# Moving batch bursts and folds to other slots of a spectral-filter and GELU kernel written out slot by slot

## The chip, the cores and the metric

The kernel runs on one core of a Trainium2 chip. The metric is the device time of one execution in microseconds (us). Five engines are at work: TensorE (PE) multiplies matrices and writes its results to PSUM, VectorE (DVE) and ScalarE (ACT) read PSUM and do elementwise work, GpSimd (POOL) builds tables and issues transfers, and SyncE (SP) issues transfers. Each engine works through its own list of instructions, and semaphores tie the lists together.

## The reference

A batch of 8 sequences of 3008 tokens with 256 channels is filtered along the sequence in the frequency domain. The filtered tokens then go through a two-layer network with an exact GELU between the layers.

```python
X = np.fft.rfft(x, axis=1)                  # x: 8 x 3008 x 256
Y = X * (filt_r + 1j * filt_i)[None]        # filter: 1505 x 256
y = np.fft.irfft(Y, n=x.shape[1], axis=1)
h = y.reshape(24064, 256) @ w_in            # 256 x 2048
g = 0.5 * h * (1.0 + erf(h / sqrt(2)))
out = g @ w_out                             # 2048 x 256, float32 out
```

## The kernel before

**Two streams share the engines.** The dense stream takes the 24064 tokens in 47 tiles of 512 tokens. For a tile, `mm1` (line 634) makes 16 blocks of the hidden layer and ACT applies the GELU to each (line 637). The second product is done by a seven-product scheme on quarters of the matrices, `mm2_seven` (line 707): 112 matmuls in seven groups m = 0 to 6 of 16, numbered n = 0 to 111. DVE forms the sums of quarters which it needs: `sums_1` (line 676), `sums_2` (line 682) and `sums_3` (line 689). Group m = 2 (n = 32 to 47) needs `sums_2`: its first half needs the first call, and n = 36 needs the second. DVE also adds up the results out of PSUM: after m = 0 (line 722), m = 2 (lines 724, 727), m = 4 (lines 729, 730, 733) and m = 6 (line 736). The results lie in the PSUM pool `o`, which has two banks. A new bank is taken at m = 0, m = 1, m = 3 and m = 5, so the bank that m = 1 of a tile takes at n = 16 must first have been emptied by line 736 of the tile before it.

The other stream filters the batches, by a transform of 3008 = 47 x 64 points in stages. For each batch b from 1 to 7:
- `fold` (lines 106, 107), four calls: DVE adds and subtracts the two halves of a quarter of the loaded input.
- `s1` (line 428), four bursts of 8 matmuls; DVE (line 331) and ACT (line 329) each copy two of the four PSUM banks to `a_sb`; SP stores it to a scratch array R in DRAM, and `r1` (line 444) loads it back in another order as `b_sb`.
- `s2` (line 457), three bursts u = 0 to 2 of 16 matmuls; `s2_out` (line 469), four calls for each burst: DVE multiplies the four banks by the filter F into `p`.
- `s3` (line 483), three bursts; it reads what the four `s2_out` calls of its u wrote. ACT empties its four banks into `v_sb` (line 329), half with the burst and half one slot later in `s3_out`; SP stores `v_sb` to a second scratch array (line 496), and `r2` (line 503) loads it back as `d_sb`.
- `s4` (line 512), sixteen bursts of 4 matmuls, numbered by a group u = 0 to 7 and a half; ACT or DVE puts the result into the ring of tokens `y_sb`, which `mm1` reads.
Bursts take one bank of the PSUM pool `h` and three of the pool `f`, which has three banks.

**The order is written out by hand.** No planner reorders the work: the kernel runs under a manual schedule. A loop runs over slots s = 0, 1, 2, ..., 16 slots for each tile. In a slot the loop first calls what has been put there with `put(slot, function, ...)`, in the order of the `put` calls; then 7 matmuls of `mm2_seven` for the tile before (tile t - 1); then one `mm1` of tile t. So each engine's list follows the slots. In the slots of tile 0 there is only `mm1` beside the bursts. Tile 5 (slots 80 to 95) needs the first tokens of batch 1; there the loop does 14 matmuls of `mm2_seven` in each of the first six slots, and starts with `mm1` at slot 86.

The plan for batch b is made around `hi = first(b)`, the first slot of the tile that needs the batch's first token: 80 for b = 1, 176 for b = 2, 656 for b = 7. `s1`, `n1`, `r1` are the first slot of the s1 bursts, their distance and the slot of `r1`; `s2` holds the three slots of the s2 bursts. The s2_out calls follow at +0, +2, +4, +6, s3 at +10 and s3_out at +11. `load_next` puts the loads of the next batch's input (POOL, line 98) behind s2_out calls of this batch: a small copy on POOL, the gate (line 149), waits for the `p` of an s2_out. `after[b]` is the slot of the first `r2`, and `busy` holds slots which s4 bursts keep clear of.

For batch 1 the s4 bursts of u = 0 lie at slots 83 and 84 and those of u = 1 at 86 and 87. The stores of tiles 0 to 2 go through SP and those of later tiles through POOL. Batch 0 goes another way, before slot 0, which begins at about 38.0 us.

Of the kernel before, what the change touches and what calls it, by code (L numbers as in the profile page):

```python
# [775 lines left out]
def kernel(  # L776
# [9 lines left out]
    m = _Mix(ctx, tc, x, filt_r, filt_i, moe_w_in, moe_w_out, out)  # L786
    nc, B, S = tc.nc, m.B, m.S
# [116 lines left out]
    def put(slot, f, *a):  # L904
        at.setdefault(slot, []).append((f, a))

    def first(b):
        return (b * S // TCH) * 16

    busy, crowd, after = set(), set(), {}  # L910
    for b in range(1, B):
        hi = first(b)
        e = 4 * (b == B - 1)
        s1, n1, r1 = (1, 4, 16) if b == 1 else (hi - 87, 3.7, hi - 73) if b == 2 else (hi - 94 - e, 3.7, hi - 80 - e)
        s2 = (32, 46, 58) if b == 1 else (hi - 64 - 2 * e, hi - 48 - 3 * e, hi - 32 - 3 * e)
        busy.update(range(s1 - 1, s1 + int(3 * n1) + 2))
        for c in range(4):
            slot = s1 + int(c * n1)
            put(slot - 1 if b == 1 else s1 - 28 + 6 * c, m.fold, b, c)
            put(slot, m.s1, b, c)  # L920
            put(r1 if c < 3 else s2[0] + 1, m.r1, b, c)
        for u in range(3):
            put(s2[u], m.s2, b, u)
            for i in range(4):
                put(s2[u] + 2 * i, m.s2_out, b, u, i // 2, i % 2)
            put(s2[u] + 10, m.s3, b, u)
            put(s2[u] + 11, m.s3_out, b, u, 1)
            busy.update(range(s2[u] - 1, s2[u] + 5), range(s2[u] + 9, s2[u] + 12))
        after[b] = s2[2] + 15
        crowd.update(range(s2[0], after[b]), range(s1 + 66, s1 + 94))  # L930
        if b + 1 < B:
            for i, (u, o, p) in enumerate(((0, 5, 2), (0, 7, 2), (1, 1, 4), (1, 5, 6), (1, 7, 6), (2, 1, 8), (2, 5, 10), (2, 7, 10))):
                put(s2[u] + o, m.load_next, b, p, i // 2, i % 2)

    for b in range(1, B):
        end = 1000000
        if b == B - 1:
            s4 = first(b) - 17
            for u in range(16):
                put(s4 + u, m.s4, b, u // 2, u % 2, act if u % 2 else False)  # L940
            for c in range(4):
                put(after[b] if c < 3 else s4 + 5, m.r2, b, c)
            continue
        for u in range(7, -1, -1):
            due = (b * S + GRP * u) // TCH * 16
            end = min(end, due - 2 + 6 * (u == 0 and b == 1))
            for half in (1, 0):
                while end in busy:
                    end -= 1
                assert end > after[b] + 7  # L950
                put(end, m.s4, b, u, half, act if half or end in crowd or b == 1 and u == 0 else False)
                busy.add(end)
                end -= 1 if u < 3 else 2
            if u % 2 == 0:
                put(after[b] if u == 0 else end - 11, m.r2, b, u // 2)
# [8 lines left out]
    for i, slot in enumerate((10, 80, 96, 112)):  # L964
        put(slot, m.table_4_all, parts[2 * i:2 * i + 2])
    put(1, m.load_filters_again, nc.gpsimd, 0, 8)
    put(17, m.load_filters_again, nc.sync, 8, 16)
    put(19, m.weight_sums)
    seven = range(1, NT)
    for t in seven:  # L970
        for i, s in enumerate((12, 13, 15, 16 if t == S // TCH - 1 else 17)):
# [49 lines left out]
```

## Time and profile before

| what | value |
|---|---|
| time, median of 3 runs | 751.81 us (750.87 to 752.24) |
| the profiled execution | 750.82 us, span 749.0 us |
| PE busy | 724.9 us (97%) |
| DVE busy | 581.7 us (78%) |
| ACT busy | 574.7 us (77%) |
| POOL busy | 287.6 us (38%) |
| granted TensorE clock | full throughout |
| HBM traffic | 141 GB/s over the span |

PE's busy share is a share of the whole span. The matmuls overlap one another, so it doesn't say how near PE is to its peak; it says that PE seldom stands still. What matters here is where it does: the view of waits names, for each engine, the engine and line that ended its idle time, and the timeline shows the instructions around such a wait. A wait in one place may have its cause in a long queue on the engine that ended it.

### The profile page before, as it was taken

What the parts mean: (1) busy time and instruction counts of PE and PEld (TensorE: products, weight loads), DVE (VectorE), ACT (ScalarE), POOL (GpSimd) and SP (SyncE); (2) the same over time, 40 slices, a digit from 0 to 9 for tenths busy, and PEclk for the clock granted to TensorE, in tenths of its full rate; (3) what the DMA queues carried; (4) which work ended last, traced back from release to release, by engine and by line L of the source; (5) the groups of instructions that cost most, each with busy time, mean ns of one, the idle gap of its engine ahead of it and who ended that gap; (6) DMA issues with size and microseconds to landing.
All of it is one profiled execution on the core that took longest, in us unless ns stands there. A gap on an engine that the chain in (4) does not pass through costs nothing.

```text
span 749.0 us, 20863 instructions
## 1 busy us (share of the span) xinstructions
PE 724.9 (97%) x8450; PEld 507.4 (68%) x8588; DVE 581.7 (78%) x1034; ACT 574.7 (77%) x1050; POOL 287.6 (38%) x540
## 2 busy tenths in 40 slices
PE   7989999999999999999999999999999999999997
PEld 4846665666777667666677666666667766777776
DVE  7976797888887788778976889768887887676566
ACT  6986776777887788778887777877778787777773
POOL 7894325676122553134521354115531121112121
PEclk9999999999999999999999999999999999999999
DMA  9999652746346653656436456265545442401011
GB/s 148 221 208 222 144 117 74 208 106 124 86 116 182 121 115 87 154 139 135 105 108 169 107 117 152 71 156 136 110 101 127 143 111 84 111 30 57 30 58 57
DMA packets 84378, 90.79 MB, mean 121 GB/s; under 512 B 13290, under 2 KB 63466, under 8 KB 84154
## 3 DMA queue, kind: packets, MB, share of 16 engines
q1 hardware_dynamic: 61594, 49.63, 26.1%
q0 software_dynamic: 22272, 39.63, 23.9%
q8 instruction: 67, 1.10, 0.7%
q14 instruction: 29, 0.24, 0.1%
q10 hardware_dynamic: 416, 0.20, 0.1%
HBM read 57.15 MB, written 48.23 MB: 141 GB/s over the span
## 4 chain that ended last, share of the span: by engine, by line
PE 84%; ACT 5%; DVE 3%; DMA 3%; issue 2%; POOL 1%; DVEq 0%; SPq 0%; POOLq 0%
PE ps_o L707 36%; PE ps_h L634 36%; PE ps_s L483 3%; ACT g_sb L637 3%; PE ps_s L512 3%; PE ps_s L428 2%; DMA x_sb<-in_x_dram 2%; PE ps_s L457 1%; ACT v_sb L329 1%; PE ps_o L648 1%; DVE s_sb L676 1%; DMA F<-in_filt_i_dram 1%; ACT y_sb L329 1%; DMA b_sb<-R 1%; PE ps_c L581 0%
## 5 line engine op out<-in xcount | busy, mean ns | idle before, releaser
L637 ACT ACTIVATE g_sb<-ps_h 128x512 f16<-128x512 f32 x752 | 446.4, 604 | 150.9 <-PE ps_h L634 133.1
L634 PE MATMUL ps_h<-y_sb,w_in_sb 128*128 128x512 bf16 (+3 forms) x1466 | 416.5, 365 | 1.1 <-ACT g_sb L637 0.6
L754 POOL DMA_DIRECT2D out_dram<-ost x221 | 125.3, 574 | 397.7 <-DVE ost L736 389.1
L707 PEld LDWEIGHTS <-g_sb 128*128 128x128 f16 x2944 | 193.4, 98 | 87.6 <-issue 11.2
L707 PEld LDWEIGHTS <-s_sb 128*128 128x128 f16 x2208 | 147.9, 98 | 62.2 <-issue 11.3
L707 PE MATMUL ps_o<-w_sums,g_sb 128*128 128x128 f16 x1472 | 127.9, 219 | 3.1 <-DVE g_sb L682 2.2
L634 PEld LDWEIGHTS <-w_in_sb 128*128 128x128 bf16 x1600 | 124.9, 98 | 8.6 <-issue 2.5
L707 PE MATMUL ps_o<-w_sums,s_sb 128*128 128x128 f16 x1472 | 126.0, 219 | 1.8
L676 DVE TENSOR_TENSOR s_sb<-g_sb 128x1024 f16<-128x1024 f16 x184 | 120.4, 688 | 3.3 <-ACT g_sb L637 3.3
L707 PE MATMUL ps_o<-w_out_sb,g_sb 128*128 128x128 f16 x1472 | 119.1, 219 | 3.5 <-DVE ost L736 1.9
L469 DVE TENSOR_TENSOR p<-ps_s,F 128x1024 bf16<-128x1024 f32 x84 | 102.5, 1220 | 6.7 <-PE ps_s L457 5.3
L98 POOL DMA_DIRECT2D x_sb<-in_x_dram x156 | 79.0, 513 | 0.7 <-PE ps_c3t L596 0.4
L729 DVE TENSOR_TENSOR t_sb<-t_sb,ps_o 128x256 f32<-128x256 f32 x46 | 19.4, 421 | 64.9 <-PE ps_o L707 64.8
L682 DVE TENSOR_TENSOR g_sb<-s_sb,g_sb 128x1024 f16<-128x1024 f16 x92 | 65.1, 708 | 0.7
L689 DVE TENSOR_TENSOR s_sb<-g_sb 128x1024 f16<-128x1024 f16 x92 | 64.5, 701 | 0.0
L707 PE MATMUL ps_o<-w_out_sb,s_sb 128*128 128x128 f16 x736 | 63.9, 219 | 0.4
L329 ACT ACTIVATE y_sb<-ps_s 128x376 bf16<-128x376 f32 x95 | 47.3, 497 | 5.1 <-PE ps_s L512 5.1
L736 DVE TENSOR_TENSOR ost<-t_sb,ps_o 128x256 f32<-128x256 f32 x90 | 33.8, 417 | 21.9 <-PE ps_o L707 21.9
L512 PEld LDWEIGHTS <-d_sb 96*128 96x128 bf16 x448 | 31.9, 98 | 25.5
L331 DVE CAST a_sb<-ps_s 128x512 bf16<-128x512 f32 x54 | 34.8, 686 | 16.3 <-PE ps_s L428 16.0
L329 ACT ACTIVATE v_sb<-ps_s 128x512 bf16<-128x512 f32 x84 | 45.5, 597 | 0.2
L724 DVE TENSOR_TENSOR ost<-t_sb,ps_o 128x256 f32<-128x256 f32 x46 | 19.2, 418 | 26.9 <-PE ps_o L707 26.9
(154 smaller groups left out, 523.9 us busy)
## 6 DMA issues: line engine op xcount, KB each, us to landing
out_dram<-ost POOLq DMA_DIRECT2D x123, 128.0 KB, 2.7
b_sb<-R SPq DMA_DIRECT2D x28, 384.0 KB, 4.3
R<-v_sb SPq DMA_DIRECT2D x84, 128.0 KB, 2.4
d_sb<-R SPq DMA_DIRECT2D x56, 192.0 KB, 4.2
R<-a_sb SPq DMA_DIRECT2D x108, 96.0 KB, 2.2
x_sb<-in_x_dram POOLq DMA_DIRECT2D x48, 94.0 KB, 2.7
x_sb<-in_x_dram POOLq DMA_DIRECT2D x48, 48.0 KB, 2.7
x_sb<-in_x_dram POOLq DMA_DIRECT2D x12, 188.0 KB, 5.1
```

Source lines behind the costliest of these rows:

```text
L98: self.nc.gpsimd.dma_start(out=xt[64 * v + to:64 * v + to + m, h, 4 * c:4 * c + 4 * n, :], in_=xv[h][at:at + m, w:w + 4 * n, :])
L329: self.nc.scalar.activation(out=out, in_=in_, func=AF.Copy, scale=1.0 if scale is None else scale)
L331: self.nc.vector.tensor_copy(out=out, in_=in_)
L469: self.nc.vector.tensor_tensor(out=self.st[b, "w"][:, :, d:4:2, :], in0=ps.unsqueeze(1).to_broadcast([128, 2, 2, 256]), in1=self.F[:, :, k ...
L512: nc.tensor.matmul(ps[:, 94 * i:94 * i + 94], lhsT=d[:, (grp % 2) * 4 + i, 128 * half:128 * half + 128], rhs=self.T4a[:, 4 * grp + i], sta ...
L634: nc.tensor.matmul(ps[:, o:o + n], lhsT=w[:, dc], rhs=self.ring[:, dc, off:off + n], start=(dc == 0), stop=(dc == 1))
L637: nc.scalar.activation(out=self.st["g", t][:, jc, :], in_=ps, func=AF.Gelu)
L676: self.nc.vector.tensor_tensor(out=self.st["s", t][:, i:i + 2], in0=a, in1=b, op=ALU.subtract)
L682: self.nc.vector.tensor_tensor(out=a21[:, k], in0=self.st["s", t][:, k, 0], in1=a22[:, k], op=ALU.add)
L689: self.nc.vector.tensor_tensor(out=self.st["s4", t][:, k], in0=a12[:, k], in1=s2[:, k], op=ALU.subtract)
L707: nc.tensor.matmul(ps[:, (m + 1) % 2, sub, :], lhsT=a[:, i, 128 * sub:128 * sub + 128], rhs=b[:, i], start=i == 0, stop=i == 7)
L754: eng.dma_start(out=out, in_=tile_[lo - r0:lo - r0 + n])
```

## The change

The work stays the same; slots and the order within the engines' lists change.

- Batch 1's s1 bursts go from slots 1, 5, 9, 13 to 2, 6, 10, 14, while their folds stay at 0, 4, 8, 12. `r1`, a reload of filters and the weight sums go one slot later.
- Batch 1's s2 bursts go from slots 32, 46, 58 to 33, 45, 57, with their s2_out calls. Its s3 bursts go from 42, 56, 68 to 42, 54, 66. The first `r2` goes from 73 to 70.
- Batch 1's s4 bursts of u = 0 and 1 go from 83, 84, 86, 87 to 80, 81, 82, 83.
- Batch 2's folds go from 61, 67, 73, 79 to 67, 69, 71, 73, behind all of batch 1's s2_out calls.
- Batch 7's folds go from 530, 536, 542, 548 to 534, 540, 546, 552.

It is meant to take DVE work out of places where PE waits for DVE, and to let PE work ahead where it waits for a fold.

```diff
-        s1, n1, r1 = (1, 4, 16) if b == 1 else (hi - 87, 3.7, hi - 73) if b == 2 else (hi - 94 - e, 3.7, hi - 80 - e)
-        s2 = (32, 46, 58) if b == 1 else (hi - 64 - 2 * e, hi - 48 - 3 * e, hi - 32 - 3 * e)
+        s1, n1, r1 = (2, 4, 17) if b == 1 else (hi - 87, 3.7, hi - 73) if b == 2 else (hi - 94 - e, 3.7, hi - 80 - e)
+        s2 = (33, 45, 57) if b == 1 else (hi - 64 - 2 * e, hi - 48 - 3 * e, hi - 32 - 3 * e)
         busy.update(range(s1 - 1, s1 + int(3 * n1) + 2))
         for c in range(4):
             slot = s1 + int(c * n1)
-            put(slot - 1 if b == 1 else s1 - 28 + 6 * c, m.fold, b, c)
+            put(slot - 2 if b == 1 else 67 + 2 * c if b == 2 else s1 - 28 + e + 6 * c, m.fold, b, c)
...
-            put(s2[u] + 10, m.s3, b, u)
-            put(s2[u] + 11, m.s3_out, b, u, 1)
-            busy.update(range(s2[u] - 1, s2[u] + 5), range(s2[u] + 9, s2[u] + 12))
-        after[b] = s2[2] + 15
+            s3 = s2[u] + (9 if b == 1 else 10)
+            put(s3, m.s3, b, u)
+            put(s3 + 1, m.s3_out, b, u, 1)
+            busy.update(range(s2[u] - 1, s2[u] + 5), range(s3 - 1, s3 + 2))
+        after[b] = s3 + (5 if b > 1 else 4)
...
-            end = min(end, due - 2 + 6 * (u == 0 and b == 1))
+            end = min(end, due - 2 if u or b > 1 else 81)
+            if b == u == 1:
+                end = 83
...
-    put(17, m.load_filters_again, nc.sync, 8, 16)
-    put(19, m.weight_sums)
+    put(18, m.load_filters_again, nc.sync, 8, 16)
+    put(20, m.weight_sums)
```

## The prediction, made before the changed kernel was run

> **What bounds the kernel now.** I read the page's first part, then PE's waits over the whole span, then the timeline around each long one. The page shows PE as the engine that almost never rests:
>
> ```profile
> PE 724.9 (97%) x8450; PEld 507.4 (68%) x8588; DVE 581.7 (78%) x1034; ACT 574.7 (77%) x1050; POOL 287.6 (38%) x540
> ```
>
> The other engines have a fifth of the span or more free, so the change can gain only where PE stands still, and what it moves between engines costs nothing unless PE comes to wait. PE's waits, longest in total first (columns: us in total, times, longest):
>
> ```profile
> PE ps_o L707 <- DVE g_sb L682: 2.2, 3, 1.2
> PE ps_o L707 <- DVE ost L736: 1.9, 2, 1.7
> ...
> PE ps_s L428 <- DVE xs L106: 0.9, 1, 0.9
> ...
> PE ps_s L457 <- ACT v_sb L329: 0.4, 2, 0.2
> ```
>
> Nearly all are waits for DVE, and few: somebody is late on DVE at six or seven places. The longest is in slot 66, where n = 16 needs the bank that line 736 empties:
>
> ```profile
> 96.50 0.69 DVE L106 TENSOR_TENSOR xs<-x_sb 111x1024 bf16<-111x1024 bf16 x1
> 97.22 0.69 DVE L107 TENSOR_TENSOR x_sb<-x_sb 111x1024 bf16<-111x1024 bf16 x1
> ...
> 98.43 1.22 DVE L469 TENSOR_TENSOR p<-ps_s,F 128x1024 bf16<-128x1024 f32 x1
> ...
> 100.16 0.75 DVE L736 TENSOR_TENSOR ost<-t_sb,ps_o 128x256 f32<-128x256 f32 x2
> ...
> 100.96 0.45 PE L707 MATMUL ps_o<-w_out_sb,g_sb 128*128 128x128 f16 x5 [1.66 <-DVE ost L736]
> ```
>
> The group that line 736 adds up was finished in slot 63, but a fold of batch 2 and s2_out calls stand before line 736 in DVE's list. Batch 7's first fold does the same to `sums_2`:
>
> ```profile
> 540.56 0.68 DVE L106 TENSOR_TENSOR xs<-x_sb 111x1024 bf16<-111x1024 bf16 x1
> ...
> 541.28 0.69 DVE L107 TENSOR_TENSOR x_sb<-x_sb 111x1024 bf16<-111x1024 bf16 x1
> ...
> 541.89 0.69 DVE L682 TENSOR_TENSOR g_sb<-s_sb,g_sb 128x1024 f16<-128x1024 f16 x1
> ...
> 542.63 0.51 PE L707 MATMUL ps_o<-w_sums,g_sb 128*128 128x128 f16 x6 [1.17 <-DVE g_sb L682]
> ```
>
> **What the Trainium skill says.** "PSUM — Partial Sum Buffer", section Engine vs sequencer instructions: the queues of ScalarE, VectorE and GpSimd are strict first in, first out, and matmuls run in program order. The trace agrees: line 736 starts 0.60 us after the item before it, never past it. "VectorE: DVE Perf Modes", section The perf-mode tier table, gives 1224 ns for a bf16 tensor_tensor of 2048 elements in SBUF; half of that for a fold's 1024 would be 0.61, and the trace has 0.68 to 0.69. "Perfetto Trace Analysis", section Identifying the Most-Contended Engine, warns that matmul busy time doesn't tell the distance to the peak; so I measure waits from start to start. One L707 matmul starts 0.055 us after another, one L634 0.215; a slot of 7 and 2 takes 0.82.
>
> **The waits, start to start.** 99.03 (two matmuls) to 100.96: 1.82 in slot 66. 541.25 to 542.63: 1.33 in slot 533. 85.19 to 85.93: 0.68 in slot 53 (`sums_2`). Slots 80 to 83: 0.43 (line 736), 0.31 and 0.72 (`sums_2`). The s2 burst of slot 58 takes 1.26 from 91.18 to the next L707, that of slot 46 takes 0.57: 0.69 lost, the banks still hold v_sb. In sum 5.98, and the start.
>
> **The change, part by part.** DVE's spacing in a full queue, from the same rows: s2_out 1.14, a fold's pair 1.33, sums 0.60, line 722 0.33, lines 724 and 727 0.79, lines 729 to 733 1.12, line 736's pair 0.66. Times below are on the trace's clock, less what was gained before.
>
> *Start.* Before, PE does one mm1 pair at 38.00 and stands until the fold's first result at 39.33. After, slot 1's pair (0.43) comes before the burst and fits into that gap; fold, copies and the later bursts stay bound by DVE and ACT, since each period of 4 slots holds the same work. When the last burst ends, PE is one pair ahead: +0.43. `weight_sums` and `r1` a slot later have no one waiting.
>
> *Slots 44 to 53.* The burst at 45 lets the first s2_out start at 78.04 + 0.46 = 78.50 instead of 79.32, but `sums_1` of slot 45 (0.60) now comes behind it. The second `sums_2` ends at 85.87 - 0.82 + 0.60 = 85.65; the wait shrinks from 0.68 to 0.46: +0.2.
>
> *s3 at 54 instead of 56.* A new wait: its second half reads the s2_out of slot 51. DVE: `sums_2` starts 84.98, line 722 85.58, s2_out 85.91 to 87.13. PE is there at 86.5 + 0.43 = 86.95: 0.2 lost. If DVE is late by another slot it is 1.0; I take 0.2. Behind it on PE everything waits, DVE doesn't.
>
> *s2 at 57.* It now lies three slots behind s3 instead of two: v_sb's last copy ended 3.6 us after s3's start (88.44 to 92.04), and the second half of the burst comes at 2.74 (88.44 to 91.18) + 0.82 + 0.32 = 3.9. The wait goes: +0.7.
>
> *Slot 66.* PE now reaches slot 57's burst at 90.3. DVE: s2_out 90.76, s2_out (slot 59) 91.9, lines 729 to 733 93.0, `sums_1` 94.15, s2_out 94.75, `sums_1` 95.9, s2_out (63) 96.5, `sums_1` 97.6, line 736 98.2 to 98.98. The fourth s2_out takes the fold's place, yet the queue begins earlier and isn't broken by waiting. PE's n = 16 comes at 99.36 (s3, 1 us, now lies before it). No wait, with 0.4 to spare: +1.8.
>
> *The four folds in 67 to 73.* From 98.9 DVE has three sums (1.8), line 722, four folds (5.3), two sums, lines 724 to 733 (1.9): it is done at 109.5, in no one's way, since the bank of line 733 is wanted at slot 80, 110.95, and `sums_3` is done at 107 for a use at 108.8. But three `sums_1`, line 736 and two `sums_2` follow, to 114.1. In slots 80 to 82 PE does 36 matmuls (2.0) and three s4 bursts (0.17 each), and wants the last `sums_2` at 113.4, and 736's bank and the first `sums_2` a bit before they are there: 0.7 to 1.1 lost, I take 1.1, against 1.46 before: +0.3.
>
> *s4 at 80.* A wait that could be added: it needs d_sb. SP's list before:
>
> ```profile
> 100.60 4.65 SPq L754 DMA_DIRECT2D out_dram<-ost  x6
> ...
> 105.35 2.47 SPq L496 DMA_DIRECT2D R<-v_sb  x4
> ...
> 109.81 0.84 SPq L503 DMA_DIRECT2D d_sb<-R  x2
> ```
>
> The stores of line 736 stand first, so all moves up by what line 736 does, 100.16 - 98.23 = 1.93: d's loads are issued at 107.9. Such a load lands in 3.0 to 5.4, median 4.2, so between 110.9 and 113.3; PE comes at 110.95. I take the lower end, as little else is moving (DMA share 0.52 from 96 to 112 us and 0.25 from 112 to 128): 0.1, inside the 1.1. The upper end would add 1.2 net.
>
> *Batch 7.* Without the fold, `sums_2` starts at 540.56 and ends at 541.24, just as PE wants it: +1.33. Behind s2_out of slot 534 the fold ends at 545.7; the next sum that PE waits on there is in slot 549, and DVE reaches it with 0.7 to spare although the fold of 546 stands before it. Its input is no concern: it didn't wait for it even four slots earlier.
>
> Sum: 0.43 + 0.2 - 0.2 + 0.7 + 1.8 + 0.3 + 1.33 = 4.5 us. 751.8 - 4.5 = 747.3.
>
> **The rivals.** *A, part is given back in slots 66 to 83:* d_sb lands late and the queue in slot 66 is half a microsecond longer than I add up. For it: d_sb has no slack at all, and 0.4 is little. Against: the moves on SP follow from line 736. 4.5 - 1.2 - 0.5 = 2.8: 749.0. *B, the s2_out takes the fold's place and nothing else:* slot 66 and slots 80 to 83 wait as before. For it: 1.14 for 1.33 is no relief in itself. Against: one slot of head start and the end of the v_sb wait. 0.43 + 0.7 + 1.33 = 2.5, less the new s3 wait at up to 1.0: 1.5, 750.3. *C, slower:* SP's list doesn't move up, d_sb is issued at 109.8 and lands after 5.4, at 115.2: PE waits 4.3 in slot 80, against 1.5 lost there before, so 2.8 more; slot 66 keeps its wait and s3 waits 1.0. Gains 0.43 + 0.7 + 1.33 + 0.2 = 2.7, losses 3.8: 752.9.
>
> **How the numbers follow.** Forecast 0.72, A 0.17, B 0.07, C 0.04. The time is the forecast's. Downwards the range takes in that the 1.1 of slots 80 to 82 goes too, 746.2; upwards A, 749.0, and a little of the three runs' spread of 1.4: 749.3. Faster by over 0.2% (under 750.3): forecast, A and a third of B, 0.90 less some doubt, 0.89; within 0.2%: 0.07; slower: 0.04.
>
> **What would show it.** In the profile after: no wait of PE for line 736 in slot 66; none at `sums_2` in slot 533; s2 of slot 57 in 0.57 us; a wait of some 0.2 in s3 of slot 54; about 1 us of waits for line 682 in slots 80 to 82. Wrong would make it a long wait of PE line 512 for d_sb in slot 80, s3 waiting for `p` by a microsecond, or folds that themselves wait for their input, with all of DVE's list behind them.

## The result, and the profile after

The changed kernel takes 746.40 us (median of 4 runs, 745.38 to 746.76), the kernel before 751.61 us beside it (4 runs, 750.87 to 752.24): ratio 0.9929, 95% interval 0.9912 to 0.9946, so 5.3 us (4.1 to 6.6) faster. A second set of runs gave 745.61 against 750.91 us, 0.9929 (0.9917 to 0.9942). The forecast was 747.3 us, with 746.2 to 749.3 as its range.

The page's first part of the changed kernel shows why busy shares can't tell the story. Every engine's busy time is within 0.4 us of what it was; only the span is shorter.

```profile
PE 724.5 (97%) x8450; PEld 507.0 (68%) x8588; DVE 581.9 (78%) x1034; ACT 575.0 (77%) x1050; POOL 287.6 (39%) x540
```

PE's waits in the changed kernel (us in total, times, longest). Line 736 has left the list, `sums_2` has gone from 2.2 to 0.8 us, and among the new lines is the wait for `d_sb`:

```profile
PE ps_o L707 <- DVE g_sb L682: 0.8, 2, 0.4
PE ps_s L512 <- DMA d_sb<-R: 0.6, 1, 0.6
...
PE ps_s L457 <- ACT v_sb L329: 0.2, 1, 0.2
```

Slot 66 in the timeline of the changed kernel (start us, us, engine, line). DVE still has an s2_out and a `sums_1` in front of line 736, but the queue begins earlier, and the s3 burst stands before PE's n = 16. Line 736 ends at 98.55; the L707 row at 98.89 starts with no wait, and n = 16, its third matmul, at 99.01, 0.46 us after line 736:

```profile
96.08 1.21 DVE L469 TENSOR_TENSOR p<-ps_s,F 128x1024 bf16<-128x1024 f32 x1
...
97.81 0.74 DVE L736 TENSOR_TENSOR ost<-t_sb,ps_o 128x256 f32<-128x256 f32 x2
97.90 1.06 PE L483 MATMUL ps_s<-p,U 64*64 64x512 bf16 x16
...
98.89 0.57 PE L707 MATMUL ps_o<-w_out_sb,g_sb 128*128 128x128 f16 x7
```

Slot 533 of the changed kernel. With the fold gone from in front of it, the call of `sums_2` that n = 36 needs runs from 536.95 to 537.63. n = 36 is the second matmul of the L707 row at 537.63, which has no wait in it:

```profile
536.95 0.68 DVE L682 TENSOR_TENSOR g_sb<-s_sb,g_sb 128x1024 f16<-128x1024 f16 x1
...
537.20 0.59 PE L634 MATMUL ps_h<-y_sb,w_in_sb 128*128 128x512 bf16 x2
...
537.63 0.56 PE L707 MATMUL ps_o<-w_sums,g_sb 128*128 128x128 f16 x7
```

The third s2 burst of batch 1, in slot 58 of the kernel before and then in slot 57 of the changed one. Before, its second part waits for `v_sb`, and the burst takes 1.25 us up to the next L707; after, it takes 0.56:

```profile
91.18 0.69 PE L457 MATMUL ps_s<-b_sb,T2p 64*64 64x256 bf16 x9
...
92.09 0.41 PE L457 MATMUL ps_s<-b_sb,T2p 64*64 64x256 bf16 x7 [0.22 <-ACT v_sb L329]
...
92.44 0.56 PE L707 MATMUL ps_o<-w_sums,s_sb 128*128 128x128 f16 x7
```

```profile
89.83 0.63 PE L457 MATMUL ps_s<-b_sb,T2p 64*64 64x256 bf16 x16
90.39 0.56 PE L707 MATMUL ps_o<-w_sums,s_sb 128*128 128x128 f16 x7
```

SP's list in the changed kernel moved up by 2.35 to 2.50 us, with line 736:

```profile
98.25 4.65 SPq L754 DMA_DIRECT2D out_dram<-ost  x6
103.00 2.47 SPq L496 DMA_DIRECT2D R<-v_sb  x4
107.31 0.84 SPq L503 DMA_DIRECT2D d_sb<-R  x2
```

Slot 80 on PE. The last `mm1` pair starts at 109.98 and needs 0.43; the s4 burst comes at 111.17, so 0.75 are lost from start to start, of which the row names 0.59:

```profile
109.98 0.59 PE L634 MATMUL ps_h<-y_sb,w_in_sb 128*128 128x512 bf16 x2
111.17 0.34 PE L512 MATMUL ps_s<-T4a,d_sb 96*128 96x94 bf16 x4 [0.59 <-DMA d_sb<-R]
```

**Where the time went.** All 752 GELUs (line 637), one for each block of the hidden layer, are numbered from 0 in both traces, 16 for each tile. The lead of the changed kernel at a GELU is how much earlier it starts than in the kernel before:

| up to | lead, us | gained since, us | second profile: lead | gained since |
|---|---|---|---|---|
| first GELU | 0.18 | | -0.49 | |
| end of tile 0 | 0.64 | 0.46 | -0.08 | 0.41 |
| end of tile 2 | 0.59 | -0.05 | -0.13 | -0.05 |
| block 63 (after slots 44 to 58) | 1.22 | 0.63 | 0.50 | 0.63 |
| block 79 (after slot 66) | 3.06 | 1.84 | 2.34 | 1.84 |
| end of tile 5 (after slots 80 to 95) | 3.48 | 0.42 | 2.76 | 0.42 |
| end of tile 7 | 3.60 | 0.12 | 2.88 | 0.12 |
| block 527 | 3.62 | 0.02 | 2.67 | -0.21 |
| block 543 (after slot 533) | 4.95 | 1.33 | 4.00 | 1.33 |
| last GELU | 4.94 | 0 | 4.00 | 0 |
| end of the span | 5.45 | 0.51 | 4.57 | 0.57 |

The gains of the stages that the change touches repeat to 0.05 us in the second profile; between tile 7 and block 527, where nothing was moved, the second profile loses 0.21 that the first doesn't. The entry (-0.7 to +0.2 us over all profiles here) doesn't follow the edits: the changed kernel itself has 0.18 and -0.49. So below, gains are read from the lead and not from the spans.

The end does follow them. From the start of the last GELU to the end of the span it is 10.24 to 10.40 us in the five profiles whose s4 bursts of u = 0 and 1 lie at slots 83 to 87, the kernel before among them; 9.68 to 9.77 in the five with these bursts at slots 80 to 84 and tile 2's stores on SP; and 10.78 and 10.79 in the two with these stores on GpSimd. In the first group SP issues the last store 7.20 us after the last GELU, in the other two 6.90. So half a microsecond of the gain stands behind the last GELU, far from any moved burst. That it belongs to the s4 slots is shown by the run that puts these bursts alone back (10.37); by what way they act on the end is not.

### The profile page after: what moved, and what is told of

The parts are those of the page before. It is cut to its first block, busy times and chain, and to the rows that moved or that the text cites. A ratio compares the mean times of both kernels' runs of the same rounds, so it can differ in the third digit from the quotient of the medians.

```text
span 743.6 us, 20861 instructions
## 1 busy us (share of the span) xinstructions
PE 724.5 (97%) x8450; PEld 507.0 (68%) x8588; DVE 581.9 (78%) x1034; ACT 575.0 (77%) x1050; POOL 287.6 (39%) x540
## 4 chain that ended last, share of the span: by engine, by line
PE 86%; ACT 5%; DVE 3%; DMA 2%; issue 2%; POOL 0%; SPq 0%; DVEq 0%; POOLq 0%
PE ps_o L707 37%; PE ps_h L634 36%; PE ps_s L483 3%; ACT g_sb L637 3%; PE ps_s L512 3%; PE ps_s L428 2%; PE ps_s L457 2%; ACT v_sb L329 1%; DMA x_sb<-in_x_dram 1%; PE ps_o L648 1%; DVE s_sb L676 1%; PE ps_c L581 1%; DVE g_sb L682 1%; DMA F<-in_filt_i_dram 1%; ACT y_sb L329 1%
## 5 line engine op out<-in xcount | busy, mean ns | idle before, releaser
L707 PEld LDWEIGHTS <-g_sb 128*128 128x128 f16 x2944 | 193.1, 98 | 84.0 <-issue 11.8
L707 PEld LDWEIGHTS <-s_sb 128*128 128x128 f16 x2208 | 148.0, 98 | 62.1 <-issue 10.7
L707 PE MATMUL ps_o<-w_sums,g_sb 128*128 128x128 f16 x1472 | 127.8, 219 | 1.9 <-DVE g_sb L682 0.8
L707 PE MATMUL ps_o<-w_sums,s_sb 128*128 128x128 f16 x1472 | 125.9, 219 | 1.7
L707 PE MATMUL ps_o<-w_out_sb,g_sb 128*128 128x128 f16 x1472 | 119.1, 219 | 1.6
L707 PE MATMUL ps_o<-w_out_sb,s_sb 128*128 128x128 f16 x736 | 63.9, 219 | 0.4
```

Source lines behind the costliest of these rows:

```text
L707: nc.tensor.matmul(ps[:, (m + 1) % 2, sub, :], lhsT=a[:, i, 128 * sub:128 * sub + 128], rhs=b[:, i], start=i == 0, stop=i == 7)
```

## The experiments

The first four each make one part of the change alone on the kernel before; the others change the changed kernel.

**Batch 7's folds alone**

```diff
-            put(slot - 1 if b == 1 else s1 - 28 + 6 * c, m.fold, b, c)
+            put(slot - 1 if b == 1 else s1 - 28 + e + 6 * c, m.fold, b, c)
```

> The kernel before with batch 7's folds alone moved, from slots 530, 536, 542, 548 to 534, 540, 546, 552. Theory (the fold stood before sums_2 in DVE's list): PE's wait of 1.33 us in slot 533 is gone and none replaces it, the span is 1.3 us shorter, all else as before. Rival (DVE is full for two tiles and the fold is only put off): a wait of 0.5 us or more turns up at the sums_2 of slot 549, gain 0 to 0.8 us.

Measured: 749.81 us (15 runs) against 751.13 (46 runs), ratio 0.9985 (0.9977 to 0.9992). The lead is 0.02 up to block 111 and steps up by 1.33 in slot 533; slot 549 has no wait. About 0.17 were lost elsewhere, in s2 of batch 2 (slot 112), which waits for its loads of `b_sb` at another moment. This part is what the prediction said: 1.33 us, whole.

**Batch 1's first bursts alone**

```diff
-        s1, n1, r1 = (1, 4, 16) if b == 1 else ...
+        s1, n1, r1 = (2, 4, 17) if b == 1 else ...
...
-            put(slot - 1 if b == 1 else s1 - 28 + 6 * c, m.fold, b, c)
+            put(slot - 2 if b == 1 else s1 - 28 + 6 * c, m.fold, b, c)
...
-    put(17, m.load_filters_again, nc.sync, 8, 16)
-    put(19, m.weight_sums)
+    put(18, m.load_filters_again, nc.sync, 8, 16)
+    put(20, m.weight_sums)
```

> The kernel before with batch 1's s1 bursts alone at slots 2, 6, 10, 14, and r1, the filter reload and the weight sums one slot later. Theory (PE does one mm1 pair while it would stand before the fold): PE leads by 0.43 us from slot 2 on and keeps it, span 0.4 us shorter. Rival (VectorE and ScalarE bound the stretch, the pair is waited for later): lead gone by slot 16, no gain. A run cannot show 0.4 us in its time; the trace can, by the GELU of slot 15.

Measured: 750.61 us (13 runs), ratio 0.9996 (0.9988 to 1.0004). By the median a gain of 0.5, by the interval none that this can tell. In the trace the lead goes from -0.41 at the first GELU to 0.00 at the end of tile 0, +0.41, and 0.30 is lost again further on (0.05 by the end of tile 2, as in the changed kernel, 0.11 at slot 112, 0.15 between tiles 9 and 25). The step is there; the runs are too coarse for it.

**Batch 2's folds alone**

```diff
-            put(slot - 1 if b == 1 else s1 - 28 + 6 * c, m.fold, b, c)
+            put(slot - 1 if b == 1 else 67 + 2 * c if b == 2 else s1 - 28 + 6 * c, m.fold, b, c)
```

> The kernel before with batch 2's folds alone moved, from slots 61, 67, 73, 79 to 67, 69, 71, 73. Theory (DVE's list): line 736 of slot 63 starts 1.33 us earlier, PE's wait in slot 66 falls from 1.82 to about 0.5 us; the waits in slots 80 to 83 stay at 1.5 to 1.8, since the folds only stand earlier in the same list; span 1.0 to 1.3 us shorter. Rival (the gain in slot 66 is that of the earlier bursts): the wait in slot 66 stays over 1.2 us, span the same within 0.5 us.

Measured: 750.34 us (21 runs), ratio 0.9988 (0.9982 to 0.9995). The wait in slot 66 falls from 1.82 to 0.49, +1.33. Then it loses 0.57: the four folds are one behind the other in DVE's list, which reaches line 736 of the next tile late. PE at slots 80 to 83 in this run:

```profile
114.60 1.07 PE L707 MATMUL ps_o<-w_out_sb,g_sb 128*128 128x128 f16 x16 [0.83 <-DVE ost L736]
...
116.74 0.45 PE L707 MATMUL ps_o<-w_sums,g_sb 128*128 128x128 f16 x5 [0.54 <-DVE g_sb L682]
```

From start to start 1.00 + 0.30 + 0.70 = 2.0 us, where the kernel before lost 1.42 (0.42 + 0.30 + 0.70). Of the 1.33 that the folds free in slot 66, 0.57 are paid back when tile 5 begins; 1.5 to 1.8 had been expected to be lost there, and the gain of 0.79 by the medians is short of the 1.0 to 1.3.

**The forward bursts alone** (s2, s3, r2 and s4 of batch 1; all folds as before)

```diff
-        s2 = (32, 46, 58) if b == 1 else ...
+        s2 = (33, 45, 57) if b == 1 else ...
...
-            put(s2[u] + 10, m.s3, b, u)
+            s3 = s2[u] + (9 if b == 1 else 10)
+            put(s3, m.s3, b, u)
...
-        after[b] = s2[2] + 15
+        after[b] = s3 + (5 if b > 1 else 4)
...
-            end = min(end, due - 2 + 6 * (u == 0 and b == 1))
+            end = min(end, due - 2 if u or b > 1 else 81)
+            if b == u == 1:
+                end = 83
```

> The kernel before with batch 1's s2, s3, r2 and s4 slots alone as in the changed kernel; the folds of batch 2 stay at 61, 67, 73, 79. Theory: the wait of s2 in slot 57 for the banks goes (0.7 us), s3 of slot 54 waits 0.2 to 0.3; the wait in slot 66 is still there at about 1 us, since the fold of slot 61 stands before line 736; slots 80 to 83 lose about 1.2; span 1.6 to 2.0 us shorter. Rival (the fold's move matters little, the earlier bursts do it): no wait in slot 66, span 3 us shorter.

Measured: 749.50 us (8 runs), ratio 0.9978 (0.9968 to 0.9988). Slots 44 to 58 gain 0.63, exactly as in the changed kernel, so they owe nothing to the folds. Slot 66 still waits 0.58 for line 736, and s3 in slot 66 takes 1.33 instead of 0.99, another 0.34. What the theory missed is in slot 80, at PE's first s4 burst:

```profile
114.33 0.33 PE L512 MATMUL ps_s<-T4a,d_sb 96*128 96x94 bf16 x4 [2.06 <-DMA d_sb<-R]
```

2.22 us are lost there. SP issues the loads of `d_sb` at 109.36, 2.05 later than in the changed kernel, since line 736 is late in slot 66. And they take longer to land: 4.97 from the first issue to the burst, against 3.86. In the transfers from 109 to 114 us of this run, one packet of instruction fetch (111.50 to 112.73) stands beside the load's 800. All but 25 of these are over 3.03 us after the first issue; the 25 trickle in until 113.7, 4.36 after it. In the changed kernel the fetch comes at 112.17, after the load, and the last packet is over after 3.14.

```profile
q1 hardware_dynamic: 800, 0.39, 33.9%
q8 instruction: 1, 0.02, 1.5%
```

The profiles agree with the fetch as the cause: in one more, that of the run with s4 in pairs, a fetch falls into the middle of this load, and there its last packet is over after 4.10; in the ten others, where the fetch starts in the last 0.5 us of the load or later, after 2.90 to 3.14. No run takes the fetch away alone, so it is likely, not shown. What is shown is that slot 66's wait isn't local: when line 736 is late, the stores, R and `d_sb` behind it on SP are late by as much.

**The changed kernel with s4 of u = 0 and 1 late** (slots 83, 84, 86 and 87, as before)

```diff
-            end = min(end, due - 2 if u or b > 1 else 81)
+            end = min(end, due - 2 if u or b > 1 else 84)
             if b == u == 1:
-                end = 83
+                end = 87
```

> The changed kernel with batch 1's s4 bursts of u = 0 and 1 back at slots 83, 84, 86, 87. Theory (the wait for d_sb in slot 80 hides behind DVE's list, which is late for sums_2 anyway): the d_sb wait of 0.75 us is gone, but PE then waits for line 736 and sums_2 in slots 80 to 83, 1.5 to 1.7 us instead of 1.06 in all; span 0.5 us longer than the changed kernel's. Rival (the d_sb wait is a plain loss): span 0.7 us shorter.

Measured: 747.29 us (5 runs) against 751.18 (9 runs), ratio 0.9944 (0.9930 to 0.9957). The wait for `d_sb` is gone, and nothing is gained by that. PE meets DVE instead:

```profile
112.66 1.07 PE L707 MATMUL ps_o<-w_out_sb,g_sb 128*128 128x128 f16 x16 [0.42 <-DVE ost L736]
...
114.80 0.51 PE L707 MATMUL ps_o<-w_sums,g_sb 128*128 128x128 f16 x6 [0.54 <-DVE g_sb L682]
```

From start to start 0.59 + 0.30 + 0.70 = 1.59, where the changed kernel loses 1.06; over tile 5 the lead goes from 2.29 to 2.13, 0.58 worse than the changed kernel's +0.42. The first theory held for this stage; a further 0.6 lies at the end of the span (10.37 against 9.75). So the early bursts are worth half a microsecond even though they wait for their input: their 0.17 us each and their wait both fall into time that PE would lose to DVE anyway.

**The changed kernel with two of batch 2's folds later** (67, 69, 84, 90; the s4 bursts at 81 to 84)

```diff
-            put(slot - 2 if b == 1 else 67 + 2 * c if b == 2 else s1 - 28 + e + 6 * c, m.fold, b, c)
+            put(slot - 2 if b == 1 else (67, 69, 84, 90)[c] if b == 2 else s1 - 28 + e + 6 * c, m.fold, b, c)
...
-            end = min(end, due - 2 if u or b > 1 else 81)
+            end = min(end, due - 2 if u or b > 1 else 82)
             if b == u == 1:
-                end = 83
+                end = 84
```

> The changed kernel with batch 2's third and fourth fold at slots 84 and 90 instead of 71 and 73, and the s4 bursts of u = 0 and 1 at 81 to 84 instead of 80 to 83. Theory: DVE's list before slot 80 is 2.66 us shorter, so line 736 and sums_2 are in time, and d_sb has landed before slot 81; the waits of slots 80 to 83 fall from 1.06 to 0.3 us or less, span 0.8 us shorter than the changed kernel's. Rival (the two folds meet the sums of tile 5 in slots 85 to 95): as much is lost there, no gain.

Measured: 746.97 us (5 runs), ratio 0.9937 (0.9925 to 0.9950). Tile 5 gains 0.70 in the lead instead of 0.42: 0.28 better, not 0.8. The waits for `d_sb` and for line 736 are gone, but 0.70 at the second `sums_2` stay. DVE isn't behind there. Its rows show a chain that starts with a wait for ACT:

```profile
111.98 0.69 DVE L676 TENSOR_TENSOR s_sb<-g_sb 128x1024 f16<-128x1024 f16 x1 [0.31 <-ACT g_sb L637]
112.59 0.68 DVE L682 TENSOR_TENSOR g_sb<-s_sb,g_sb 128x1024 f16<-128x1024 f16 x1
113.20 0.42 DVE L722 COPY t_sb<-ps_o 128x256 f32<-128x256 f32 x1
113.53 0.68 DVE L682 TENSOR_TENSOR g_sb<-s_sb,g_sb 128x1024 f16<-128x1024 f16 x1
```

The last GELU of tile 4 ends at 111.95, and from there to the end of the second `sums_2`, at 114.21, nothing can be shortened by moving folds. The rival is out: from slot 84 to slot 111 the lead loses nothing.

**The same folds with the s4 bursts in pairs** (81, 81, 82, 82; this edit besides that of the folds, on the changed kernel)

```diff
-                put(end, m.s4, b, u, half, act if half or end in crowd or b == 1 and u == 0 else False)
+                put(81 + u if b == 1 and u < 2 else end, m.s4, b, u, half, act if half or end in crowd or b == 1 and u == 0 else False)
```

> The changed kernel with batch 2's folds at 67, 69, 84 and 90, and batch 1's four fourth bursts two to a slot, at 81 and 82. Theory one: what is left at slots 82 and 83 (0.70 us in the run with two folds later) is the fixed chain from the GELU of slot 79 over sums_1, the two sums_2 and line 722; PE gets there too early, and the bursts that now all lie before n = 36 fill the gap: the wait falls to about 0.36, 0.3 us better than the run with two folds later and 0.6 better than the changed kernel: about 745.8. Theory two: a pair of bursts in one slot starves the GELUs, and the next L707 waits for one: a new wait for line 637 of 0.3 to 0.5 us, nothing gained.

Measured: 747.14 us (5 runs) against 750.91 (9 runs), ratio 0.9943 (0.9930 to 0.9955). Missed. The wait at `sums_2` is gone, but the pair needs `d_sb` in slot 81, and waits 1.15 for it (issued at 108.38, with the late packets named above). Then PE loses a further 0.9 before block 86, for line 331: the copy of an s1 bank stands behind the fold of slot 84 on DVE. The run before has the same fold in the same place and loses nothing there. The difference is how long the fold takes, beside table work on GpSimd (line 412 runs from 116.61 to 117.59, line 410 from 117.66 to 120.64):

```profile
116.80 1.33 DVE L106 TENSOR_TENSOR x_sb<-x_sb 111x1024 bf16<-111x1024 bf16 x1
...
118.16 1.20 DVE L107 TENSOR_TENSOR x_sb<-x_sb 111x1024 bf16<-111x1024 bf16 x1
```

From the fold's start to the next DVE row it is 2.48, in the run before 2.00, where a fold's pair elsewhere takes 1.33. The 1.15 too much are enough for the 0.9; no run takes the table work away. No wait for a GELU showed; both theories were wrong about what comes next.

**The changed kernel with tile 2's stores on GpSimd**

```diff
-                                      nc.gpsimd if t > 2 else nc.sync)
+                                      nc.gpsimd if t > 1 else nc.sync)
```

> The changed kernel with tile 2's stores issued on GpSimd instead of SP. Theory one: SP issues the load of d_sb at 107.3 only because tile 2's stores and r2 stand before it in SP's list; without the stores it is issued about 2.5 us earlier, the wait for d_sb in slot 80 (0.75 us) goes, and PE then meets the late sums_2 and line 736 instead: the waits of slots 80 to 83 stay at 1.0 to 1.1 us in sum and the time is the same within 0.3 us. Theory two: the wait for d_sb is a cost of its own: 0.75 us better, about 745.6. Theory three: the load is issued as late as before, since what holds it is r2 and the copies of v_sb, not the stores.

Measured: 747.02 us (5 runs), ratio 0.9946 (0.9932 to 0.9960); the changed kernel on the same chip 0.9929 (0.9917 to 0.9942). SP in this run:

```profile
99.74 2.88 SPq L496 DMA_DIRECT2D R<-v_sb  x4
106.73 0.83 SPq L503 DMA_DIRECT2D d_sb<-R  x2
```

The stores to R go out 3.26 us earlier, but the load of `d_sb` only 0.58, not 2.5: it must wait until R has landed, and R's median from issue to landing is now 3.4 us instead of 2.3. That was enough to clear slot 80, and PE then waits 0.67 for line 736 and 0.12 and 0.70 for `sums_2`, 1.49 in sum, where the changed kernel waits 0.75 + 0.31. The first theory was wrong on when the load goes out and right on what PE meets next, with 0.4 more of a loss than it said; the second, a cost of its own, is out; the third is right that something else holds the load, but it is R's landing. The run's median is no measure of this stage: in its profile 1.03 us are lost behind the last GELU (10.78 against 9.75), and 0.55 are a single wait for `sums_2` in tile 25, which the changed kernel's profiles don't have.

**The changed kernel again**, beside these two:

> The changed kernel again, beside the two others on the same chip: 746.4 +- 0.4, the wait for d_sb in slot 80 at 0.75 us and 1.06 us in sum in slots 80 to 83. If d_sb lands at another time than in the first profile, the sum of the waits should still be near 1.1 as long as it lands before 112.

Measured: 745.61 us (5 runs), ratio 0.9929. Slot 80 waits 0.70 for `d_sb`, slots 80 to 83 lose 1.06 in sum. The table above has its lead.

**All three at once** (stores on GpSimd, s4 at 81, 81, 82, 82, batch 2's folds at 67, 69, 87, 92)

```diff
-                                      nc.gpsimd if t > 2 else nc.sync)
+                                      nc.gpsimd if t > 1 else nc.sync)
...
-            put(slot - 2 if b == 1 else 67 + 2 * c if b == 2 else s1 - 28 + e + 6 * c, m.fold, b, c)
+            put(slot - 2 if b == 1 else (67, 69, 87, 92)[c] if b == 2 else s1 - 28 + e + 6 * c, m.fold, b, c)
...
-                put(end, m.s4, b, u, half, act if half or end in crowd or b == 1 and u == 0 else False)
+                put(81 + u if b == 1 and u < 2 else end, m.s4, b, u, half, act if half or end in crowd or b == 1 and u == 0 else False)
```

> The changed kernel with three edits at once: tile 2's stores issued on GpSimd (as in the run with the stores moved), the four fourth bursts at 81, 81, 82 and 82, and batch 2's folds at 67, 69, 87 and 92. Theory one: three causes end within a microsecond of each other in slots 80 to 83 (the load of d_sb, line 736 behind the folds, the chain of sums behind the GELU of slot 79), and taking away one only uncovers the next; with all three eased the waits of slots 80 to 83 come to 0.4 us or less instead of 1.06, the two folds so late no longer push line 331 back, and from slot 79 to slot 95 the lead grows by 0.6 to 0.7 us more than with the changed kernel: about 745.8. Theory two: moving the work always uncovers another wait of the same size: no better than the changed kernel, 746.4 or above.

Measured: 747.84 us (5 runs) against 751.60 (9 runs), ratio 0.9959 (0.9946 to 0.9973): by the median 1.4 us worse than the changed kernel, whose interval just touches this one. In the profiles 1.04 of that is the longer end (10.79 against 9.75). In slots 80 to 83 the first theory held, 0.40 us lost instead of 1.06. But PE loses 0.52 before block 86, for line 331 behind the fold of slot 87, whose pair takes 2.12 here beside line 410, not 1.33, and 0.89 in slot 101, for a `sums_2`. DVE there, first in this run, then in the changed kernel:

```profile
127.92 1.28 DVE L331 CAST a_sb<-ps_s 128x512 bf16<-128x512 f32 x2
...
130.44 2.56 DVE L682 TENSOR_TENSOR g_sb<-s_sb,g_sb 128x1024 f16<-128x1024 f16 x1
```

```profile
127.36 1.29 DVE L331 CAST a_sb<-ps_s 128x512 bf16<-128x512 f32 x2 [0.23 <-PE ps_s L428]
...
129.88 2.24 DVE L682 TENSOR_TENSOR g_sb<-s_sb,g_sb 128x1024 f16<-128x1024 f16 x1
```

With the fold of slot 92 ahead, DVE comes to line 331 at 127.92 instead of 127.36, and the long `sums_2` lasts 2.56 instead of 2.24: 0.56 + 0.32 = 0.88, the wait. In the changed kernel the same stretched call ends just as PE wants it. So in the lead, too, the second theory is right for the whole: room made in slots 80 to 83 was paid for in slots 86 to 101. None of these versions beats the changed kernel by its runs; two folds later alone comes nearest, 0.28 better in tile 5, with nothing paid for it, and not to be told apart by its runs.

## Why the prediction was right

It said 4.5 us by seven steps (its terms add up to 4.56); the trace shows 4.68 for the same steps (0.46 + 0.63 + 1.84 + 0.42 + 1.33, the second for three of them). Most of the rest of the 5.3 of the runs is at the end of the span, 0.51 and 0.57 in the two profiles, which no step foresaw. So the time came out 0.2 above the lower end of the range, and not for the reason that the range gave: the loss in slots 80 to 82 was still there. Without the half microsecond at the end the forecast would have met the time more closely; that part is no merit or fault of its argument. Point by point:

| step | forecast | measured |
|---|---|---|
| start | +0.43 | +0.46 (alone +0.41) |
| `sums_2` of slot 53 | wait 0.46 | 0.58 (before 0.68) |
| s3 at 54, new wait | 0.2 | 0.16 (1.15 instead of 0.99) |
| s2 at 57 | +0.7 | +0.69, no wait left |
| these three together | +0.7 | +0.63 |
| slot 66 | +1.8, 0.4 to spare | +1.84, 0.46 to spare |
| slots 80 to 83 | 1.1 lost, of it 0.1 for `d_sb` | 1.06 lost, of it 0.75 for `d_sb` |
| batch 7 | +1.33 | +1.33 (alone +1.33) |

- *Slot 66* was the largest term, and its working holds row by row, all rows about 0.4 us earlier than put: the first s2_out at 90.36 (put at 90.76), line 736 at 97.81 to 98.55 (98.2 to 98.98), PE's n = 16 at 99.01 (99.36). It needs both parts. The folds alone leave 0.49 of the wait; the forward bursts alone leave 0.58 and 0.34 more at s3. One fold fewer or one slot earlier isn't enough; together they end 0.46 before PE.
- *Slots 80 to 83* came out right in sum though one of its terms was mis-sized. The loads of `d_sb` were put at 107.9 and issued at 107.31; the burst came 3.86 after that, where the lower end, 3.0, had been taken. This cost nothing, because DVE wasn't ready either: 0.75 for `d_sb` took the place of most of the 1.0 for `sums_2` and line 736. Without the wait for `d_sb` the loss was 1.49 (stores on GpSimd) and 1.59 (late s4 bursts). The clause "inside the 1.1" was the right one; "the upper end would add" more holds too, as the forward bursts alone show with 2.22.
- *Rival A* (part is given back in slots 66 to 83) is what the folds alone and the forward bursts alone do: 0.57 and 0.73 given back there. In the whole change it didn't happen: line 736 moved SP's list up, so that `d_sb` came 2.05 earlier than with the forward bursts alone, and the early s4 bursts fill time that PE loses to DVE with the folds alone. *Rival B* (s2_out takes the fold's place) is refuted by slot 66; *rival C* (`d_sb` issued at 109.8) by SP's list.
- *Not foreseen*: 0.12 at slots 112 to 117. The kernel before waits there for `b_sb` (0.80 from start to start); the changed one waits 0.08 for it but loses 0.59 at a `sums_2` that lasts 1.35, beside line 410 on GpSimd.

The four parts measured singly give 1.32 + 0.52 + 0.79 + 1.63 = 4.3 us by their medians; together they give 5.2. The fourth has 0.56 of its 1.63 at the end of the span. The traces show where they don't add up: in slot 66 the folds alone gain 1.33 and the forward bursts alone 0.90, together 1.84, less than their sum; in slots 80 to 83 both lose when alone (0.57 and 0.73) and gain 0.42 together.

## What to carry to other kernels

In a list written out by hand, take the long waits of the engine that never rests, and count the items queued in front of the instruction each of them waits for; moving one item out of that queue pays in full where the next wait is far away (batch 7), and only in part where several queues come due within a microsecond. There, price the stage as a whole: the latest of the rivals sets the end, removing it uncovers the next, and a wait that lies beside another one costs nothing. Before moving work into a "free" stretch, look at who comes due behind it; here folds put behind slot 83 cost nothing in one run and were paid for by a copy or a sum some slots later in two, according to what ran beside them on GpSimd.

## What the runs showed of the hardware

- **DVE's sums can stretch while GpSimd runs line 410.** In the changed kernel 368 calls of lines 676, 682 and 689 have the same shape. Of the 360 that don't overlap a call of line 410 on GpSimd (an f32 multiplication of tiles in SBUF), all but one last about 0.68 us, and the one, 1.23, lies beside line 412. The 8 that do overlap last 0.83 to 2.24. Folds do the same where they meet it (1.33 and 1.20 in the run with pairs, 0.96 and 1.20 in the run with all three). The overlap isn't enough by itself: over the other profiles 7 sums last 0.68 to 0.69 although they overlap line 410 by 0.47 to 0.68 us. The Trainium skill, "SBUF — State Buffer", section Who interferes with whom, says that a DVE instruction with two SBUF inputs contends with a GpSimd instruction that reads SBUF. The trace agrees in direction; the row of 2.24 lies beside these on GpSimd in the changed kernel, and ends within line 412:

```profile
129.95 1.61 POOL L410 TENSOR_TENSOR tmp_sb<-t_sb 96x376 f32<-96x376 f32 x2
131.64 1.32 POOL L412 TENSOR_TENSOR T4a<-tmp_sb 96x376 bf16<-96x376 f32 x1
```

- **A load can depend on how fast the store before it lands.** With the stores to R issued 3.26 us earlier, but beside the output stores on the other queue, R's landing took 3.4 instead of 2.3 us, and the reload gained only 0.58. That the stores beside it slow R down is not shown.
- **The entry varies by 0.67 us between two profiles of the same kernel**, more than the smallest steps here are worth. The end repeats to 0.07 in these two and differs by up to 1.1 between kernels whose last instructions do the same work (9.68 to 10.79). A lead measured between numbered instructions inside the run repeats to 0.05 us over the steps of this change.
